# Batch 1's convolution on VectorE, batch 4's q by DMA transpose, convolution buffers of one batch, and a new written-out order

## The chip, the core and the metric

The kernel runs on one core of a Trainium2 chip. A core has five engines with an instruction queue each: TensorE (PE, with its weight loads as PEld), VectorE (DVE), ScalarE (ACT), GpSimd (POOL) and SyncE (SP). Each runs its own instructions in order; they wait for each other by semaphores. Transfers run on 16 DMA engines that POOL's and SP's queues share. The metric is the time of one execution on the device in microseconds (us).

## The reference

```python
kv  = einsum('bhsd,bhse->bhde', k, v)         # 8 batches, 8 heads, 576 rows, 64 wide
out = einsum('bhsd,bhde->bhse', q, kv)
x   = out / sqrt(mean(out * out, -1) + 1e-6) * g_norm   # heads side by side: 576 x 512
h   = maximum(x @ w_in, 0)                    # 576 x 1024
conv = conv_w[0] * h[s-1] + conv_w[1] * h[s] + conv_w[2] * h[s+1]   # along the rows
result = (h * sigmoid(conv)) @ w_out          # 576 x 512, float32
```

q, k, v and the weights arrive as float32 in HBM; the kernel computes in bfloat16 and sums in float32.

## The kernel before, in words

All eight batches pass through the same steps, and the steps of different batches lie beside each other. The program is one list of tokens, `ORDER` (from line 67). A loop at the end of the kernel calls one small function for each token, in the order of the list, so that the list fixes each engine's own order of instructions. A token is the function's name with its arguments (`hm.2.5`: batch 2, slice 5), `@` and the numbers of the buffers it takes, and `:1` or `:0`, which chooses between ScalarE and VectorE where a function has both.

The steps of a batch b, with their functions and the lines of their instructions:

- `Lq`, `Lk`, `Lv` (L301): POOL issues a load of the whole batch, 576 KB in bfloat16, cast on the way. Each of q, k and v has two buffers in turn, by the number behind `@`, so a load waits until what was in its buffer has been read (q of 7 takes the buffer of q of 4). `Li` and `Lo` (L315, L322) load the weights.
- `kv` (L358): 48 matmuls for k by v, with tiles of 128 by 64. `kvc` (L341, L343) copies the result out; from batch 4 on it is `kvn`, and the half that has to change partitions comes by a second copy (`ky`) or by DMA (`kx`, L449).
- q transposed. Batches 0 to 3: `qt` (L380) on TensorE, then a copy `qc`. Batch 4: `qtp`, the same step through `by_parity`, 24 transposes of two heads' worth each (L388), then `qc` on VectorE. Batches 5, 6, 7 (`QD`, line 60): `dq`, two DMA transposes a batch, four heads each, that SP issues (L436); no TensorE, no copy.
- out: `ot` (L430, L431) for batches 0 to 3, `oq` (L464) from batch 4 on, with tiles of 64 by 64, one for each pair of heads. `oq.b.0` and `oq.b.1` need the transpose `dq.b.0`; `oq.b.2` and `oq.b.3` need `dq.b.1`.
- the norm: `sq` squares (ScalarE), `oc` copies out, `ss` (L575, tiles of 128 by 32) sums, `ln` and `sl` make the factors, `sp` (L603, tiles of 32 by 128) spreads them, `mu` (L629) multiplies into x. Batch 7 spreads them through HBM instead (`fw`, `fr`).
- `hm` (L640): 8 matmuls of 288 columns for each of 8 slices of h; `re` evicts one with the maximum (L646 on ScalarE, L648 on VectorE).
- the convolution, in groups of batches (`CONV`, line 64): 0 and 1 alone, then 2 with 3, 4 with 5, 6 with 7. `ta` (L699, L700) makes the two outer taps, `aa` (L706) and `ab` (L712) add, all on VectorE; `sg` (L745) takes the sigmoid on ScalarE; `mg` (L751) multiplies it into h on VectorE. For slices 6 and 7 of batches 0 and 1 the convolution is instead a matmul with diagonal weights, `cm` (L731), and `sg` reads its result (L742). The buffers are two tiles `taps`, each for two slices of two batches.
- `om` (L761): h by w_out, 128 rows and 8 matmuls of 512 columns for each output row block; `ea` evicts it, `st` (L795) stores it through SP. The last block is done in halves (`oh`, L776).

`unread` (L427) runs matmuls on a constant whose result nobody reads.

Around the change, SP's queue is in the order of its tokens: transposes, `kx`, factors and stores. POOL's queue holds all loads in one line.

Of the kernel before, what the change touches and what calls it, by code (L numbers as in the profile page):

```python
# [72 lines left out]
sqh.0.3.0@3 unread.3@3 onh.0.3.0@6 sqh.0.3.1 onh.0.3.1 nlh.0.3.0@3 muh.0.3.0 Lk.1.0@1 qt.1.0@0 nlh.0.3.1 qc.1.0:1@2
muh.0.3.1 Li.0 hm.0.2@6 re.0.2 ta.0.2@0 hm.0.3@4 re.0.3 hm.0.6@6 Lq.1.2 ta.0.3 Lv.1.2 re.0.6 aa.0.1 hm.0.7@4 Lk.1.2
Lq.2.0@0 cm.0.6@6 re.0.7:1 sg.0.6@1 kv.1.0.2@0 cm.0.7@4 kvc.1.0.2.0:1@1 kvc.1.0.2.1 sg.0.7 ot.1.0@0 hm.0.1@6 ab.0.1
sq.1.0@4 re.0.1 qt.1.1@4 hm.0.0@2 on.1.0@6 mg.0.3 qc.1.1@3 ot.1.1@4 nl.1.0@4 re.0.0:1 sq.1.1@5 kv.1.2.2@2
kvc.1.2.2.0 ta.0.0@1 mu0.1.0 kvc.1.2.2.1 on.1.1@6 Li.2 ot.1.2@2 nl.1.1@5 ot.1.3@0 ta.0.1 sq.1.2@6 mu0.1.1 aa.0.0
unread.1@6 on.1.2@6 sq.1.3@7 ab.0.0 nl.1.2@6 mu0.1.2 on.1.3@4 nl.1.3@7 Lk.2.0@0 qt.2.0@6 sg.0.3 qt.2.1@4 mu0.1.3
ha.1.2@2 hb.1.2 qc.2.1@4 sg.0.2 qc.2.0@0 ha.1.3@0 hb.1.3 re.1.2 re.1.3 hm.1.7@4 Lv.2.0@0 hm.0.4@2 mg.0.1 Lq.3.0@1
hm.0.5@0 sg.0.1 Lk.3.0@1 Lv.3.0@1 re.1.7 sg.0.0 pl ta.1.2@0 re.0.4 ta.1.3 re.0.5 hm.1.4@4 kv.2.0.4@2 Lo.0 aa.1.1  # L80
ab.1.1 mg.0.0 sg.1.3 sg.1.2 kvc.2.0.4.0@0 hm.1.5@0 kvc.2.0.4.1 ta.0.4@1 ta.0.5 ot.2.0@2 mg.1.1 aa.0.2 hm.1.6@6
re.1.4 ot.2.2@4 re.1.5 sq.2.0@0 ta.1.4@0 ab.0.2 re.1.6 qt.3.1@0 oc.2.0:1@0 qt.3.0@6 qc.3.1@1 hm.1.1@2 ot.2.1@0
# [35 lines left out]
om.3.0.0@4 st.2.3 ea.3.6@6 ea.3.1@0 st.3.6 st.3.3 st.3.1 st.2.4 st.2.5 om.3.5.4 om.3.2.4 om.3.7.0@2 st.2.6 ea.3.4@6
st.2.0 eh.3.8.0@7 st.3.4 om.3.0.4 ea.3.5@0 om.3.7.4 oh.3.8.1 ea.3.2@3 ea.3.0@4 ea.3.7@1 st.3.5 st.1.4 sh.3.8.0
st.3.2 st.3.0 st.3.7 eh.3.8.1 sh.3.8.1  # L120
"""


# [722 lines left out]
```

## Time and profile before

| | us |
|---|---|
| median of 3 runs (179.9 to 182.42) | 180.41 |
| span of the profiled execution | 177.6 |
| around it, to the median | 2.8 |
| PE busy | 168.4 |
| ACT busy | 149.7 |
| DVE busy | 139.5 |
| POOL busy | 30.8 |

The span runs from the first to the last instruction. "Busy" is the time in which the engine had an instruction in work. The profile's rows of digits cut the span in 40 slices of 4.4 us and give the busy share of each in tenths. The chain of waits follows the work that ended last back to what released it. In the timeline a row stands for instructions in sequence: start, time, engine, line and operation, and their number; the duration of a single matmul overlaps with the next one's, so that what a matmul adds is read from starts, or from the chain. For a transfer, "to landing" is the time from its issue to its last byte. The rows of DMA queues give packets, megabytes, and the time of the packets as a share of 16 engines: q0 holds POOL's casting loads, q1 what SP issues.

### The profile page before, as it was taken

To read this page: it belongs to the slowest core of one execution; us is meant where nothing else is said; L and a number is where in the kernel's file an instruction comes from. 1 tells how busy PE (TensorE), PEld (TensorE's weight loads), DVE (VectorE), ACT (ScalarE), POOL (GpSimd) and SP (SyncE) were. 2 spreads that over 40 slices of the span, in tenths; PEclk is the share of its full clock that TensorE was granted. 3 is DMA by queue.
4 is the path that set the end of the run, shared out by engine and by line. 5 is a ranking of instruction groups with operands and counts; after the bars stand their busy time and mean duration, and the time that the engine had idled before them with its cause. 6 is when DMAs were issued, how large, how long until landed. Compare 5 with 4: busy or idle time off the path is not lost.

```text
span 177.6 us, 4060 instructions
## 1 busy us (share of the span) xinstructions
PE 168.4 (95%) x1641; PEld 101.3 (57%) x1660; DVE 139.5 (79%) x235; ACT 149.7 (84%) x233; POOL 30.8 (17%) x54
## 2 busy tenths in 40 slices
PE   6989996999999999999999999999999999999992
PEld 2545753877545677753667764444677764444541
DVE  5665669999998898999799999939999999950000
ACT  2479899999999969999999999999989987764332
POOL 7995516402600013050000000000000000000000
PEclk9999999999999999999999999999999999999999
DMA  6999999999999999999999950197040003422696
GB/s 155 188 183 197 200 204 201 205 203 206 205 204 203 198 192 139 174 203 198 160 201 179 293 128 0 53 219 263 21 160 0 4 0 143 152 82 99 258 352 219
DMA packets 36219, 29.49 MB, mean 166 GB/s; under 512 B 8528, under 2 KB 31720, under 8 KB 36200
## 3 DMA queue, kind: packets, MB, share of 16 engines
q0 software_dynamic: 21760, 15.96, 59.5%
q1 hardware_dynamic: 14400, 13.26, 28.9%
q8 instruction: 13, 0.21, 0.4%
q14 instruction: 6, 0.05, 0.1%
q10 hardware_dynamic: 40, 0.01, 0.0%
HBM read 33.70 MB, written 9.58 MB: 244 GB/s over the span
## 4 chain that ended last, share of the span: by engine, by line
PE 70%; DMA 20%; POOL 4%; ACT 2%; issue 2%; POOLq 0%; ACTq 0%
PE bank L761 33%; PE bank L640 27%; DMA v_sb<-in_v_dram 10%; DMA k_sb<-in_k_dram 7%; DMA q_sb<-in_q_dram 4%; PE bank L358 3%; PE bank L464 2%; POOL q_sb L241 1%; PE bank L603 1%; PE bank L575 1%; POOL v_sb L241 1%; POOL k_sb L241 1%; PE bank L776 1%; PE bank L731 1%; PE bank L388 1%
## 5 line engine op out<-in xcount | busy, mean ns | idle before, releaser
L640 PE MATMUL bank<-xT,w_in_sb 128*128 128x288 bf16 x496 | 64.5, 286 | 0.1
L761 PE MATMUL bank<-w_out_sb,h 128*128 128x512 bf16 x268 | 63.0, 379 | 1.1 <-issue 0.6
L640 PEld LDWEIGHTS <-w_in_sb 128*128 128x128 bf16 x496 | 47.6, 98 | 14.1 <-issue 0.5
L761 PEld LDWEIGHTS <-h 128*128 128x128 bf16 x280 | 26.3, 98 | 30.6 <-issue 1.9
L646 ACT ACTIVATE h<-bank 128x576 bf16<-128x576 f32 x61 | 37.9, 657 | 4.2 <-PE bank L640 3.9
L745 ACT ACTIVATE taps<-taps,cwn 128x1152 bf16<-128x1152 bf16 (+1 forms) x36 | 38.2, 1094 | 0.1
L341 ACT ACTIVATE row<-bank 128x512 f32<-128x512 f32 (+1 forms) x37 | 21.3, 598 | 12.3 <-PE bank L761 9.3
L751 DVE TENSOR_TENSOR h<-h,taps 128x2304 bf16<-128x2304 bf16 (+1 forms) x20 | 22.2, 1113 | 2.0 <-ACT taps L745 1.2
L706 DVE TENSOR_TENSOR taps<-taps 128x2304 bf16<-128x2304 bf16 (+1 forms) x18 | 20.9, 1160 | 0.4
L712 DVE TENSOR_TENSOR taps<-taps,h 128x2304 bf16<-128x2304 bf16 (+1 forms) x18 | 20.8, 1153 | 0.3
L699 DVE TENSOR_SCALAR taps<-h,cwn 128x1152 bf16<-128x1152 bf16 (+1 forms) x36 | 16.7, 463 | 2.5 <-ACT h L646 2.4
L493 ACT ACTIVATE sq<-bank 128x576 bf16<-128x576 f32 x28 | 17.9, 676 | 0.0
L700 DVE TENSOR_SCALAR taps<-h,cwn 128x1152 bf16<-128x1152 bf16 (+1 forms) x36 | 17.5, 487 | 0.0
L629 DVE SCALAR_TENSOR_TENSOR xT<-o,cw,bank 128x576 bf16<-128x576 f32 x20 | 15.3, 809 | 2.7 <-PE bank L603 2.5
L341 ACT ACTIVATE o<-bank 128x576 f32<-128x576 f32 x22 | 15.0, 694 | 0.0
L213 ACT ACT_TABLE_LOAD x10 | 12.8, 1283 | 2.5 <-issue 2.4
L301 POOL DMA_DIRECT2D q_sb<-in_q_dram x8 | 6.2, 772 | 31.4 <-PE bank L388 16.6
L427 PE MATMUL bank<-fill 128*128 128x512 bf16 x25 | 9.0, 480 | 1.7 <-DVE fill L228 1.5
L358 PEld LDWEIGHTS <-k_sb 96*64 96x64 bf16 x384 | 7.3, 114 | 4.0 <-issue 2.6
L358 PE MATMUL bank<-v_sb,k_sb 96*64 96x64 bf16 x384 | 8.5, 199 | 1.0 <-DMA k_sb<-in_k_dram 0.7
L301 POOL DMA_DIRECT2D k_sb<-in_k_dram x8 | 6.1, 758 | 14.4 <-PE bank L358 12.5
L562 DVE SCALAR_TENSOR_TENSOR xT<-bank,cw,root 128x576 bf16<-128x576 f32 x7 | 5.6, 815 | 1.8 <-ACT root L542 1.7
(93 smaller groups left out, 135.3 us busy)
## 6 DMA issues: line engine op xcount, KB each, us to landing
out_dram<-row SPq DMA_DIRECT2D x35, 256.0 KB, 2.8
q_sb<-in_q_dram POOLq DMA_DIRECT2D x6, 576.0 KB, 13.7
k_sb<-in_k_dram POOLq DMA_DIRECT2D x6, 576.0 KB, 14.7
v_sb<-in_v_dram POOLq DMA_DIRECT2D x6, 576.0 KB, 16.3
factor<-factor SPq DMA_DIRECT2D x4, 288.0 KB, 4.9
w_in_sb<-in_moe_w_in_dram POOLq DMA_DIRECT2D x4, 256.0 KB, 8.7
w_out_sb<-in_moe_w_out_dram POOLq DMA_DIRECT2D x2, 512.0 KB, 18.0
q_sb<-in_q_dram POOLq DMA_DIRECT2D x4, 144.0 KB, 4.6
```

The lines of the kernel that those rows point to most:

```text
L341: nc.scalar.activation(to, fr, AX.Copy)
L358: nc.tensor.matmul(ps[i][i * D:(i + 1) * D, t - t0, :], k_sb[:, 2 * t + i, r * D:(r + 1) * D], v_sb[:, 2 * t + i, r * D:(r + 1) * D], star ...
L493: nc.scalar.activation(in_order(b, s), product(b, t), AX.Square)
L640: nc.tensor.matmul(ps[:, e, :HS], w_in_sb[:, t, f * P:(f + 1) * P], x[:, t, e * HS:(e + 1) * HS], start=(t == 0), stop=(t == NT - 1))
L646: nc.scalar.activation(to, fr, AX.Relu)
L699: nc.vector.tensor_scalar_mul(tap[:, 0, f % 2, :n, 8:8 + S], h[:, f], cwn[:, 0, f:f + 1])
L700: nc.vector.tensor_scalar_mul(tap[:, 1, f % 2, :n, :S], h[:, f], cwn[:, 2, f:f + 1])
L706: nc.vector.tensor_add(tap[:, 1, :, :n, :S], tap[:, 0, :, :n, 7:7 + S], tap[:, 1, :, :n, 1:1 + S])
L712: nc.vector.tensor_add(y, y, h[:, 2 * j:2 * j + 2])
L745: nc.scalar.activation(y, y, AX.Sigmoid, scale=cwn[:, 1, f:f + 1])
L751: nc.vector.tensor_mul(h, h, T["tap", c, j][:, 1, :, :n, :S])
L761: nc.tensor.matmul(T["om", p, m], h[:, f, m * P:(m + 1) * P], w_out_sb[:, f, :], start=(f == 0), stop=(f == NF - 1))
```

## The change

Three edits, and a new `ORDER` for all of the list.

- Batch 1's convolution of slices 6 and 7 is done as the other slices are, by `ta`, `aa` and `ab` on VectorE; the tokens `cm.1.6` and `cm.1.7` go.
- Batch 4 joins `QD`: its q is transposed by two DMAs, `dq.4.0` and `dq.4.1`; the tokens `qtp.4.0`, `qtp.4.1`, `qc.4.0` and `qc.4.1` go.
- The two tiles `taps` for two batches become four units for one batch each; a group of one batch takes one unit, a group of two takes two that lie side by side.

The new list also moves work between ScalarE and VectorE by the `:` choices (16 evictions of `hm` on VectorE, before 3; seven output rows there, before none), places 25 instead of 27 `unread` matmuls, and changes TensorE's tile shape 71 times instead of 80. Loads stand in the order v4, k4, q4, q5, k5, v5, q7, k6, v6, k7, v7, q6 (before: q4, q5, k4, v4, k5, v5, q7, v7, k7, k6, v6, q6), and SP's queue begins with `dq.4.1`, `dq.4.0`, `dq.5.0`, `st.0.3`, `dq.5.1` (before: `dq.5.0`, `dq.5.1`, `st.0.0`, `dq.7.0`).

```diff
-QD = (5, 6, 7)
-QP = (4,)
+QD = (4, 5, 6, 7)
+QP = ()
...
+    def units(n):
+        s = slots.pop(0)
+        return taps[:, s:s + n].rearrange("p b k f w -> p k f b w")
...
-    taps = [consts.tile([P, 2, 2, 2, TW], BF16, name=f"taps{i}") for i in range(2)]
+    taps = consts.tile([P, 4, 2, 2, TW], BF16, name="taps")
...
-        for t in taps:
-            nc.vector.memset(t[:, 0, :, :, 7:8], 0.0)
-            nc.vector.memset(t[:, 1, :, :, S:S + 1], 0.0)
+        nc.vector.memset(taps[:, :, 0, :, 7:8], 0.0)
+        nc.vector.memset(taps[:, :, 1, :, S:S + 1], 0.0)
...
-            T["tap", c, f // 2] = taps[slots.pop(0)]
+            T["tap", c, f // 2] = units(CONV[c][1])
...
-                T["tap", c, f // 2] = taps[slots.pop(0)]
+                T["tap", c, f // 2] = units(CONV[c][1])
```

Of the list, the stretch around batch 4 and the line with `kv.7`:

```diff
-dq.5.0@3 ea.0.1@0 mu.2.1.0 Lk.5.0@1 mu.2.1.1 om.0.0.4 ea.0.3@1 ln.1@0 sp.2.0@4,6 mu.2.0.1 mu.2.0.0 dq.5.1@0
-om.0.2.0@2 Lv.5.0@1 sg.1.5 sg.1.4 qtp.4.0@0 cm.1.6@6 qc.4.0@4 mg.1.2 ea.0.0@2 hm.2.5@4 sl.1@0 hm.2.2@0 sg.1.1
...
-mu.4.1.1 sp.4.0@4,0 kv.7.0.4@6 mu.4.0.0 sg.2.2 mu.4.0.1 om.0.7.4 kvn.7.0.4:1 sg.2.3 ea.0.7@2 sp.5.0@4,2 hm.3.0@0
...
+om.0.3.0@0 mu.2.0.1 mu.2.1.0 dq.4.1@2 al.x2@0 mu.2.1.1 sl.1@0 om.0.3.4 ea.0.3@3 hm.2.2@4 kv.4.0.4@0 sg.1.2 ab.1.3
+re.2.2 sp.3.0@2,6 mu.3.0.0 sg.1.4 sg.1.7 Lq.5.0@1 mu.3.0.1 hm.2.6@4 kvn.4.0.4 ky.4.0.4.0 ky.4.0.4.1 Lk.5.0@1 re.2.6
+sg.1.6 hm.2.3@2 hm.2.7@6 aa.1.0 sp.3.1@0,4 re.2.3:1 dq.4.0@0 hm.2.5@2 ab.1.0 dq.5.0@1 Lv.5.0@1 st.0.3 re.2.7 sg.1.1
+sg.1.5 mu.3.1.1 hm.2.4@6 re.2.5 mu.3.1.0 mg.1.3 dq.5.1@3 hm.3.4@4 re.2.4:1 oq.4.2@0 sg.1.0 mg.1.2 re.3.4 sq.4.2@0
...
+st.0.2 sp.4.0@0,4 kv.6.0.4@3 kv.7.0.4@7 mu.4.0.0 mu.4.0.1 sg.2.2 sp.4.1@0,4 ea.0.7@1 kvn.6.0.4:1 hm.2.1@2 mu.4.1.0
```

More of the change, by code (lines that the diff above doesn't have):

```diff
@@ L73 @@
[L73 to L82, printed above, removed]
@@ L118 @@
[L118 to L120 removed]
+pre@0,0,0 ca.v.0 unread.10@6 qt0.0.0@0 ca.k.0 kv.0.0.1@1 kvc.0.0.1.0@0 kvc.0.0.1.1:1 qc0.0.0:1@0 pi Lq.1.0@1 Li.3
+qt0.0.1@2 unread.2@6 ot.0.0@4 kv.0.1.1@3 al.h1@0 ct@0 sq.0.0@0 on.0.0@6 kvc.0.1.1.0:1 qc0.0.1:1 nl.0.0@0 pg unread.2@0
@@ new lines @@
+qt0.0.2@1 al.h0@1 al.x0@0 Li.1 kvc.0.1.1.1:1 ot.0.1@2 pc sq.0.1@0 unread.3@6 kv.0.2.1@0 on.0.1@6 qc0.0.2@1 nl.0.1@1
+mu0.0.0 kvc.0.2.1.0:1 pn Lv.1.0@1 kvc.0.2.1.1 dg.6:1 unread.2@4 qt0.0.3@1 mu0.0.1 ot.0.2@4 unread.2@7 kv.0.3.1@0,6
+sq.0.2@0 Lk.1.0@1 on.0.2@2 qc0.0.3 kvc.0.3.1.1:1 kvc.0.3.1.0 Li.0 ot.0.3@0 Lk.1.2 nl.0.2@0 sqh.0.3.0@0 sqh.0.3.1
+unread.3@6 onh.0.3.0@6 Lq.1.2 onh.0.3.1 mu0.0.2 dg.7:1 nlh.0.3.0@1 qt.1.0@2 muh.0.3.0 nlh.0.3.1 muh.0.3.1 hm.0.7@4
+qc.1.0@0 hm.0.6@0 Lv.1.2 hm.0.2@2 re.0.6:1 ps hm.0.3@6 re.0.7 Li.2 Lk.2.0@0 cm.0.6@0 kv.1.0.2@4 re.0.2:1 re.0.3:1
@@ new lines @@
+sg.0.6@0 kvc.1.0.2.0@0 kvc.1.0.2.1 cm.0.7@2 ta.0.2@1 ot.1.0@0 ta.0.3 al.x1@1 aa.0.1 sg.0.7 sq.1.0@0 hm.0.0@4 hm.0.1@2
+mg.0.3 on.1.0@6 re.0.0:1 nl.1.0@0 re.0.1 Lv.2.0@0 qt.1.1@4 ot.1.1@6 kv.1.2.2@2 ab.0.1 sq.1.1@0 Lq.2.0@0 qc.1.1@1
+on.1.1@4 kvc.1.2.2.0 kvc.1.2.2.1 ot.1.3@2 ta.0.0@0 mu0.1.0 nl.1.1@1 Lq.3.0@1 ot.1.2@0 pl hm.0.4@4 sq.1.3@0 Lv.3.0@1
+Lk.3.0@1 ta.0.1 sq.1.2@1 mu0.1.1 on.1.2@6 nl.1.2@0 re.0.4:1 on.1.3@4 mu0.1.2 hm.0.5@6 ha.1.2@0 nl.1.3@1 mu0.1.3
+hm.1.5@4 aa.0.0 ta.0.4@2 sg.0.3 re.0.5 sg.0.2 hm.1.4@2 hm.1.0@6 ab.0.0 Lo.0 hb.1.2 ta.0.5 re.1.4:1 hm.1.1@2 re.1.5
@@ new lines @@
+re.1.2 qt.2.1@0 kv.2.0.4@4 aa.0.2 Lo.1 ab.0.2 sg.0.1 sg.0.0 re.1.0:1 sg.0.4 kvc.2.0.4.0@0 qt.2.0@6 qc.2.1@0 Lv.4.0@0
+re.1.1 kvc.2.0.4.1 ha.1.3@0 mg.0.0 hb.1.3 ot.2.2@2 qc.2.0@1 sg.0.5 sq.2.2@0 hm.1.7@4 ot.2.0@6 oc.2.2@0 sq.2.0@1
+oc.2.0@1 mg.0.1 re.1.3:1 hm.1.6@0 qt.3.1@2 re.1.6 ot.2.1@6 ta.1.4@3 ot.2.3@0 re.1.7 ta.1.5 Lk.4.0@0 ta.1.0@0 qt.3.0@4
+mg.0.2 sq.2.1@2 sq.2.3@3 qc.3.1@1 ta.1.2@1 ss.2@2 ta.1.3 ln.8@0 unread.1@3 kv.3.0.4@3 kvc.3.0.4.0@0 kvc.3.0.4.1
+ot.3.2@2 qc.3.0@0 aa.1.2 oc.2.1:1 ot.3.1@4 ot.3.0@6 oc.2.3 om.0.0.0@0 om.0.1.0@1 sq.3.2@0 sq.3.0@1 aa.1.1 Lq.4.0@0
@@ new lines @@
+oq.5.3@4 sq.5.3@6 ab.2.1 sq.5.1@7 om.0.5.4 om.0.4.0@6 mg.2.2 ss.4@7 ta.2.6@2 ss.5 ea.0.6@2 om.0.8.0@0 oc.5.3 oc.5.1
+hm.3.0@4 Lv.7.0@1 ln.2@0 ta.2.7 re.3.0 ea.0.5@3 aa.2.3 sl.2@0 om.0.7.0@2 om.0.8.4 ea.0.8@4 ab.2.3 om.0.7.4 om.0.4.4
+st.0.2 sp.4.0@0,4 kv.6.0.4@3 kv.7.0.4@7 mu.4.0.0 mu.4.0.1 sg.2.2 sp.4.1@0,4 ea.0.7@1 kvn.6.0.4:1 hm.2.1@2 mu.4.1.0
+sg.2.3 mu.4.1.1 al.h2@1 dq.7.1@4 hm.4.2@0 mg.2.1 dq.7.0@0 ea.0.4@5 re.2.1 kvn.7.0.4 kx.6.0.4.0 sp.5.1@4,2 hm.4.1@6
+re.4.2 mu.5.1.1 kx.7.0.4.0 hm.4.3@0 kx.6.0.4.1 sg.2.6 hm.4.5@2 mu.5.1.0 re.4.1 re.4.3 Lq.6.0@1 re.4.5 sp.5.0@0,4
@@ new lines @@
+hm.4.0@6 ta.2.0@0 ta.2.1 hm.4.4@2 mu.5.0.1 mu.5.0.0 re.4.0 kx.7.0.4.1 hm.5.2@4 aa.2.0 hm.4.7@0 sg.2.7 ab.2.0 mg.2.3
+hm.5.3@6 re.5.2 hm.5.1@4 re.4.4 re.4.7 hm.5.0@0 sg.2.1 re.5.3:1 oq.7.0@2 sg.2.0 re.5.1:1 re.5.0 oq.7.1@6 hm.5.5@4
+hm.5.4@0 mg.2.0 ta.3.2@2 st.0.6 sq.7.0@0 oc.7.0@0 re.5.4:1 re.5.5 sq.7.1@1 om.1.0.0@2 oc.7.1 ta.3.3 aa.3.1 dq.6.0@1
+oq.7.2@0 ea.1.0@2 st.0.8 oq.6.0@4 sq.7.2@2 oq.7.3@6 ab.3.1 oc.7.2:1@1 om.1.3.0@3 om.1.6.0@2 sq.7.3@3 sq.6.0@4
+ea.1.3:1@4 dq.6.1@2 oc.7.3 oq.6.3@0 ea.1.6:1@6 st.1.0 oq.6.2@6 oc.6.0@2 ta.3.4@0 sg.3.3 oq.6.1@4 om.1.5.0@3 sq.6.1@5
@@ new lines @@
+sq.6.3@6 ss.7@2 sq.6.2@7 oc.6.1:1 oc.6.2@3 ta.3.5 sg.3.2 oc.6.3 ln.4@0 ss.6@4 st.0.4 hm.4.6@6 re.4.6 ea.1.5@2
+om.1.1.0@5 fw.4 st.1.5 aa.3.2 hm.5.7@0 mg.3.1 om.1.2.0@2 ea.1.1@5 ta.3.0@2 ta.3.1 hm.5.6@6 re.5.7 al.x3@1 ab.3.2
+om.1.8.0@3 ln.3@0 sl.3@0 fr.7.0@0 re.5.6 sp.6.0@0,4 aa.3.0 mu.6.0.0 mu.6.0.1 ea.1.2@2 om.1.7.0@2 sp.6.1@0,6 ea.1.8@7
+om.1.4.0@3 mu.7.0.0 mu.6.1.0 fr.7.1@1 mu.6.1.1 hm.6.0@0 mu.7.1.1 mu.7.1.0 st.1.6 sg.3.4 hm.6.6@4 ab.3.0 sg.3.5 al.h3@0
+mu.7.0.1 st.0.5 mg.3.2 ea.1.4@3 st.1.4 re.6.0 hm.6.2@0 re.6.6 hm.6.1@4 hm.6.3@6 re.6.2 ea.1.7@3 ta.3.6@0 sg.3.1 re.6.3
@@ new lines @@
+st.1.8 ta.3.7 hm.6.4@0 hm.7.3@2 re.6.4 re.7.3 re.6.1 hm.7.0@0 aa.3.3 hm.6.7@2 hm.7.2@4 hm.7.7@6 sg.3.0 ab.3.3 mg.3.0
+st.1.7 st.0.0 re.6.7 re.7.2 re.7.0:1 hm.7.1@2 hm.6.5@0 sg.3.6 sg.3.7 ta.4.2@2 ta.4.3 mg.3.3 ta.4.0@0 re.7.1 ta.4.1
+hm.7.6@4 aa.4.1 ab.4.1 re.7.7 hm.7.4@2 om.2.7.0@6 re.7.6 ea.2.7@0 hm.7.5@4 re.6.5 aa.4.0 om.2.0.0@6 sg.4.2 sg.4.3
+om.2.8.0@7 st.1.1 ab.4.0 om.2.5.0@0 mg.4.1 ta.4.6@2 re.7.4 ta.4.7 om.2.3.0@1 st.1.2 aa.4.3 sg.4.1 sg.4.0 st.0.7 st.2.7
+om.2.2.0@2 om.2.6.0@3 ea.2.5@0 mg.4.0 om.2.1.0@0 ea.2.2@1 re.7.5 ea.2.8@2 ta.4.4@0 ea.2.0@3 ta.4.5 ab.4.3 aa.4.2
@@ new lines @@
+sg.4.6 om.3.7.0@2 om.2.4.0@4 ea.2.6:1@5 ea.2.1@6 om.3.4.0@5 om.3.3.0@0 sg.4.7 ea.2.4@7 st.2.6 ab.4.2 om.3.2.0@3 sg.4.5
+st.2.4 st.1.3 om.3.6.0@4 st.2.8 st.2.0 sg.4.4 om.3.1.0@6 mg.4.3 om.3.5.0@7 ea.2.3@5 mg.4.2 om.3.6.4 om.3.4.4 om.3.7.4
+ea.3.4:1@2 st.2.2 st.2.5 om.3.3.4 om.3.1.4 om.3.5.4 st.2.3 st.3.4 om.3.2.4 ea.3.3:1@0 ea.3.7@7 ea.3.6@1 ea.3.1:1@3
+st.3.3 ea.3.5@4 om.3.0.0@2 om.3.0.4 st.3.7 st.3.1 ea.3.2@2 st.3.5 oh.3.8.0@0 oh.3.8.1 eh.3.8.0@0 st.2.1 ea.3.0:1@5
+st.3.6 st.3.2 st.3.0 eh.3.8.1 sh.3.8.0 sh.3.8.1
```

43 lines of the change are left out of this document (6 added, 37 removed).

## The prediction

> **What bounds the kernel now.** Four views, in this order. The page first:
>
> ```profile
> span 177.6 us, 4060 instructions
> ...
> PE 168.4 (95%) x1641; PEld 101.3 (57%) x1660; DVE 139.5 (79%) x235; ACT 149.7 (84%) x233; POOL 30.8 (17%) x54
> ...
> PE   6989996999999999999999999999999999999992
> ...
> DVE  5665669999998898999799999939999999950000
> ...
> DMA  6999999999999999999999950197040003422696
> ...
> q0 software_dynamic: 21760, 15.96, 59.5%
> ```
>
> Two resources are full. TensorE is at 9 from the eighth slice on; the DMA engines are at 9 until slice 23 (about 100 us), and what fills them is q0, the casting loads that POOL issues. Then the chain in order of time shows where the one hands over to the other:
>
> ```profile
> 28.67 17.11 DMA v_sb<-in_v_dram
> 45.78 0.14 issue
> 45.91 0.95 PE bank L358 x48
> ...
> 63.94 0.88 PE bank L358 x48
> ...
> 88.23 0.88 PE bank L358 x48
> ...
> 96.88 0.88 PE bank L358 x48
> ```
>
> L358 is the k-by-v product of a batch (`kv`). Up to 45.8 us the chain is loads: `kv` of batch 3 starts as its v lands. After that it is TensorE to the end, and 45.9 to 174.3 holds only small gaps. The other rows are `kv` of batches 4, 7 and 6; that of 5 is at 75.96. They start late enough for their loads. The question for this change is whether that stays so. Then the transposes by DMA (L436), SP's timeline with the time that its queue took over each, and over all six the time to landing:
>
> ```profile
> 56.40 7.41 SPq L436 DMA_TRANSPOSE qT<-q_sb  x2
> ...
> 78.24 1.51 SPq L436 DMA_TRANSPOSE qT<-q_sb  x1
> ...
> 91.06 1.33 SPq L436 DMA_TRANSPOSE qT<-q_sb  x1
> ...
> 95.14 1.47 SPq L436 DMA_TRANSPOSE qT<-q_sb  x1
> ```
>
> ```profile
> DMA to landing us min/median/max: 4.2/10.7/16.0
> ```
>
> One by one, from issue to landing: 10.7 (56.4), 16.0 (58.3), 12.0 (78.2) while loads run; 5.2 (91.1) and 4.2 (95.1) when the loads are ending. Last, what one does to the loads, from the DMA view of 46 to 60 us (no transpose) and of 82 to 90 us (one, on q1):
>
> ```profile
> q0 software_dynamic: 3580, 2.85, 129.6%
> ```
>
> ```profile
> q0 software_dynamic: 1450, 1.09, 95.3%
> q1 hardware_dynamic: 1184, 0.30, 37.7%
> ```
>
> 2.85 MB in 14 us is 0.204 MB/us, so a 576 KB load (0.59 MB) needs 2.9 us. In 8 us that would be 1.63 MB; 1.09 were moved. One transpose costs the loads 0.54 MB, 2.65 us. The 15 us from 60 agree: 1.68 of 3.06 MB, 6.8 us lost to two transposes and one 256 KB store (1.3 us).
>
> **The change, part by part.** The sum is made against the profiled execution: span 177.6, and 2.8 us around it give the median of 180.4.
>
> *TensorE work removed after batch 3's `kv`.* Two `cm` of batch 1 (L731): 0.74 + 0.85 us on the chain. 24 transposes of batch 4 (L388): 0.51 + 0.62. Three fills there, of which the trace shows two (L427): 0.32 + 0.38; the new ones stand ahead of `kv`. `ss` of batch 2 goes ahead of it: 0.36. Changes of tile shape fall from 80 to 71, all nine after `kv`: on the chain eight matmuls of `om` take 1.73 us among their like, and four take 0.97, not 0.87, where another shape follows, so 0.1 us each, 0.9. Together 4.7 us. Ahead of `kv` the work grows by 0.3, and its loads land when they did, so I count 0.3 against: 4.4 us.
>
> *VectorE and ScalarE.* Two `ta` pairs, one `aa` and one `ab` for f 6 and 7 of batch 1: 4 x 0.38 + 0.76 + 0.75 = 3.0 us of VectorE; their sigmoids on ScalarE are 0.78 instead of 0.65. Two copies of q (0.75 each) leave VectorE. 13 more evictions of `hm` (net) run there at 0.75 instead of ScalarE at 0.66, seven of the 35 whole output rows too. By start-to-start intervals VectorE has 9.4 us more between `kv` of batch 3 and its last product: eight evictions 5.3, three output rows 1.8, two copies of o 1.3, and 1.0 net of batch 1's convolution against q's copies. It was idle for 9.3 us from 46 to that product's end at 158.9, so it just fits; priced as a rival. The buffers in one-batch units cost nothing by themselves: four memsets (62 ns) become two, and no shape changes. What they allow is the new order.
>
> *q of batch 4 by DMA.* Loads are now v4, k4, q4, q5, k5, v5, q7, k6, v6, k7, v7, q6. The third load after w_out landed at 59.2 before (k of batch 4: 44.2 + 15.0), so q4 lands at 59.2. Summing intervals over the new order, `oq.4.2` stands 18.3 us behind `kv` of batch 3, `oq.4.1` 22.6, `oq.5.2` 26.6, `kv` of 6 and 7 37.6 and 38.4. The old order sums to 40.5 where the trace has 42.3 (45.9 to 88.2), so I add up to 1.8 for small gaps: 65.4, 69.7, 73.8, 85.4, 86.2 us.
>
> The first transpose, `dq.4.1`, heads SP's queue: issue at 59.2, landing 10.7 later, 69.9, as q5, k5 and v5 are streaming beside it. `oq.4.2` waits 4.5 us at the head of TensorE's order, and everything behind it does. `dq.4.0` follows by between 3.1 (landings at 96.3 and 99.3) and 7.2 us (67.1 and 74.3): 73 to 77; `oq.4.1` would be at 74.2, up to 2.9 more. `dq.5.0` and `dq.5.1` queue behind: another 1 to 4 us at `oq.5.2`.
>
> SP's stores behind (`st.0.3`, `st.0.1`, `st.0.2`) and the `kx` of batches 6 and 7 are later too; the first free row buffers that are asked for 10 us and more later, the second have the 13 us to `oq.7.0` (98), and both keep that cover, since TensorE is late as well: nothing.
>
> Those waits are not yet the worst. POOL's load of q7 needs batch 4's q buffer. It waited for a transpose on TensorE until 65.7 (the 16.6 us of "POOL q_sb L301 <- PE bank L388" among the waits); now for the landing of `dq.4.0`, 73 to 77, with k6, v6, k7, v7 and q6 behind it in POOL's queue. q5 lands at 62.1, k5 and v5 after 4.1 us each (62.7 to 66.8 is what a load took beside a transpose), so v5 has landed by about 70 and the stream runs dry. The first load of the kernel landed 4.2 us after issue and its 0.15 MB move in 0.7, so data flow 3.5 us after an issue: 76.5 to 80.5. Five loads are 14.5 us, plus one to three transposes beside them (`dq.5.1`, `dq.7.1`, `dq.7.0`) at 2.65: v7 lands at 93.6 to 103. The order puts `kv` of batch 7 directly behind that of 6, at 86.2; before, the last `kv` was at 96.9 and its v landed at 92.6. I take v7 at 97, as some transposes fall into the dry stretch. TensorE is then 11 us behind (the waits at `oq` are part of it), and all that follows is TensorE work.
>
> Sum: 180.4 - 4.4 + 11 = 187.0. With v7 at 93.6 or 102: 183.5 or 192.
>
> [...]
>
> [...]
>
> **The rivals.**
> - *Faster: transposes land as the late ones did* (4.2 to 5.2 us, 3.1 apart). `dq.4.1` lands at 64, `dq.4.0` at 67, q7 is issued before v5 lands, the stream has no hole, and v7, the eighth load from 59.2, lands at 82.4 and a little more. Then only the 4.4 us count: 176.0. For it: 4.2 at 95.1. Against: all three beside running loads took over 10. It decides if `dq.4.1` lands by 65.4 and v7 by 87. 8%.
> - *A transpose takes only its bytes' share*, 1.45 us, and the stream stays fed: eight loads from 59.2 are 23.2 us, six transposes 8.7; v7 at 91.1, 4.9 us late, 180.9. Against: 0.54 MB lost in 82 to 90 us. 16%.
> - *Loads are in time, VectorE is the bound.* If it keeps all 9.3 us of idleness beside 9.4 of added work, its last product ends at 168.3 instead of 158.9, with 9.6 us of TensorE and 3.3 of tail behind: 181.2 of span, 184.0. If it keeps none, 176.0. Middle: 180. For it: VectorE's digits, nearly all 9. 11%.
> - *The waits also slow the array.* The first ten fills took 4.45 us, 0.43 each, against 0.216 later, and full pace came 5.6 us after the first: about 2.8 us lost. One such loss on top of mine: 189.8; two, 192.6. Between 46 and 174 no wait is long enough to tell. 13%.
>
> **How the numbers follow.** Mine has 52%: 187.0, its own range 183.5 to 191.5. A measurement of this kernel can tell about 2% from no change: below 176.8 is faster, above 184.0 slower. Faster: 8%. Within: 16 + 11, and 5 of mine at its lower end, 32%. Slower: 47 + 13, 60%. From 179.5 to 191.5 it leaves out the faster case and about half of the last, and takes in the others.
>
> **What would show it.** Right: L436 landings over 10 us for the first two; a PE wait for them near 65 us and another at `kv` (L358), for v_sb, near 86 to 97; POOL's q_sb waiting for a DMA, not PE; DMA digits dropping below 9 near 70 to 77; no L388 or `cm` of batch 1; PE busy some 4 us shorter. Wrong: TensorE without a gap past 46 us, or the first transpose landing within 6 us, or POOL's last loads landing by 87. If DVE idles under 3 us from 46 on while PE waits for L751, it is the third rival. Granted clock under 1.00 behind a wait: the fourth.

## The result, and the profile after

The changed kernel takes 191.38 us (median of 4 runs, 188.9 to 191.83), the kernel before 180.17 (179.9 to 182.42) on the same chip: a ratio of 1.060, 95% interval 1.052 to 1.0675. Medians and ranges here and below are of all runs of a kernel; ratios leave out a run that lies more than 1.5% above the fastest of its kernel. The profiled execution took 191.22 us, its span 189.3, 11.7 more than before.

The page of the changed kernel, with the lines that answer to those of before:

```profile
span 189.3 us, 4018 instructions
...
PE 171.4 (91%) x1622; PEld 101.5 (54%) x1622; DVE 153.6 (81%) x255; ACT 139.7 (74%) x215; POOL 30.8 (16%) x54
...
PE   6899998999899909999879999999789999999991
...
PEclk9999999999999996999966999999999999999998
DMA  6999999999999999999991900306937001006685
```

TensorE now has three thin places: a digit 0 (66 to 71 us), an 8 7 (90 to 99) and a 7 8 (132 to 142). At the first two the granted clock shows a 6, once and twice; at the third it doesn't. The DMA engines are full until 99 us (102 before). TensorE is busy for 3.0 us longer although it has 38 matmuls fewer. The half clock behind the first two (0.55 and 0.50 in the windows below) explains part of that; besides, the trace of before has records of only 1641 of its 1660 matmuls (its weight loads, PEld, count 1660), so its 168.4 us are too short. What TensorE waited for (us in total, times, longest):

```profile
PE bank L466 <- DMA qT<-q_sb: 4.3, 1, 4.3
PE bank L360 <- DMA v_sb<-in_v_dram: 2.1, 1, 2.1
```

L466 is the product `oq` of batch 4's q, L360 the product `kv` (L358 before). The chain in order of time, from 59 to 106 us (start, length, what), joins the two waits:

```profile
59.13 11.48 DMA qT<-q_sb
70.62 0.04 issue
70.66 0.44 PE bank L466 x8
71.10 5.70 PE bank L642 x32
...
79.36 16.61 DMA v_sb<-in_v_dram
95.97 0.04 issue
96.01 1.50 PE bank L360 x26
...
97.87 3.95 PE bank L642 x16
```

The transpose `dq.4.1` is issued as q of batch 4 lands (59.13) and lands itself at 70.62; v of batch 7 lands at 95.97. Sixteen matmuls of L642 (`hm`) take 3.95 us behind the second wait. At full pace they take 2.1 (below, in the run with batch 7's transposes later). The windows show the clock that was granted (start:end, length, busy time of PE, PEld, DVE, ACT and POOL, then PEclk, DMA share, GB/s):

```profile
73.00:75.40 2.40, 2.40 (x12) 1.56 (x11) 2.15 (x3) 1.67 (x4) 1.48 (x2) 0.55 0.95 115
...
95.60:99.00 3.40, 2.99 (x58) 2.23 (x58) 1.09 (x2) 0.76 (x2) 0.00 (x0) 0.50 1.42 159
99.00:102.50 3.50, 3.50 (x18) 1.88 (x17) 1.91 (x3) 1.57 (x4) 0.00 (x0) 0.51 0.15 27
```

POOL's timeline shows the load of q7 held back by a transpose, as forecast, and ScalarE's a wait that nobody forecast:

```profile
72.19 0.77 POOL L303 DMA_DIRECT2D q_sb<-in_q_dram  x1 [22.07 <-DMA qT<-q_sb]
```

```profile
139.07 0.60 ACT L343 ACTIVATE row<-bank 128x512 f32<-128x512 f32 x1 [2.78 <-DMA out_dram<-row]
```

That evacuation (`ea.1.4`) needs the row buffer that the store `st.0.5` empties, and the order issues this store on SP only behind `fr.7`, the copies of batch 7's table. `hm.6.2` needs a bank that ScalarE empties behind it. Beneath this lies a second wait at the same place: VectorE's queue has a `mu` of batch 7 ahead of two of batch 6, so it waits for that table, and TensorE waits for VectorE at `hm.6.0`:

```profile
136.02 0.82 DVE L627 SCALAR_TENSOR_TENSOR xT<-o,cw,factor 128x576 bf16<-128x576 f32 x1 [1.95 <-DMA factor<-factor]
```

```profile
PE bank L642 <- DVE xT L631: 1.5, 1, 1.5
```

Where the time went is read by setting the start of each group of matmuls in the trace against the sum of the intervals of the work ahead of it at full clock. By these sums the new order has 4.2 us less work. It falls behind them by 26.0 us to the end, the old order by 10.8. The difference of 15.2 is, in order: 0.7 up to `kv` of batch 3, 1.0 at `ot.3.2` just behind it, 4.35 at `oq.4.2`, 1.8 at half clock, 2.3 at `kv` of batch 7, 2.5 at half clock, 2.3 from `hm.6.0` to `hm.6.2` where the two waits just shown lie over each other, and small ones. 15.2 - 4.2 = 11.0, of the 11.7 that the span grew.

### The profile page after: what moved, and what is told of

It reads as the page before. It is cut to its first block, busy times and chain, and to the rows that moved or that the text cites. A ratio compares the mean times of both kernels' runs of the same rounds, so it can differ in the third digit from the quotient of the medians.

```text
span 189.3 us, 4018 instructions
## 1 busy us (share of the span) xinstructions
PE 171.4 (91%) x1622; PEld 101.5 (54%) x1622; DVE 153.6 (81%) x255; ACT 139.7 (74%) x215; POOL 30.8 (16%) x54
## 4 chain that ended last, share of the span: by engine, by line
PE 51%; DMA 31%; ACT 5%; DVE 5%; issue 3%; POOL 2%; SPq 2%; POOLq 0%; ACTq 0%
PE bank L642 24%; PE bank L763 18%; DMA v_sb<-in_v_dram 11%; DMA q_sb<-in_q_dram 9%; DMA qT<-q_sb 6%; DMA out_dram<-row 3%; PE bank L360 2%; ACT L216 1%; SPq L619 1%; DMA factor<-rs 1%; PE bank L778 1%; PE bank L466 1%; PE bank L382 1%; PE bank L733 1%; ACT root L544 1%
## 5 line engine op out<-in xcount | busy, mean ns | idle before, releaser
L642 PE MATMUL bank<-xT,w_in_sb 128*128 128x288 bf16 x496 | 68.9, 296 | 2.0 <-DVE xT L631 1.5
L763 PE MATMUL bank<-w_out_sb,h 128*128 128x512 bf16 x280 | 63.8, 379 | 0.0
L642 PEld LDWEIGHTS <-w_in_sb 128*128 128x128 bf16 x496 | 49.2, 101 | 19.8 <-issue 4.4
L747 ACT ACTIVATE taps<-taps,cwn 128x1152 bf16<-128x1152 bf16 (+1 forms) x38 | 39.8, 1075 | 3.0 <-DVE taps L714 2.9
L648 ACT ACTIVATE h<-bank 128x576 bf16<-128x576 f32 x48 | 30.4, 650 | 11.1 <-PE bank L642 10.4
L343 ACT ACTIVATE row<-bank 128x512 f32<-128x512 f32 (+1 forms) x30 | 16.9, 582 | 16.0 <-PE bank L763 6.0
L701 DVE TENSOR_SCALAR taps<-h,cwn 128x1152 bf16<-128x1152 bf16 (+1 forms) x38 | 17.8, 468 | 4.6 <-ACT h L648 4.6
L702 DVE TENSOR_SCALAR taps<-h,cwn 128x1152 bf16<-128x1152 bf16 (+1 forms) x38 | 17.9, 471 | 0.0
L343 ACT ACTIVATE o<-bank 128x576 f32<-128x576 f32 x21 | 13.6, 669 | 0.0
L650 DVE TENSOR_SCALAR h<-bank 128x576 bf16<-128x576 f32 x16 | 11.9, 751 | 2.0 <-PE bank L642 1.4
L360 PE MATMUL bank<-v_sb,k_sb 96*64 96x64 bf16 x384 | 8.9, 203 | 2.4 <-DMA v_sb<-in_v_dram 2.1
L360 PEld LDWEIGHTS <-k_sb 96*64 96x64 bf16 x384 | 7.9, 118 | 4.8 <-issue 4.5
L345 DVE COPY row<-bank 128x512 f32<-128x512 f32 x7 | 4.8, 688 | 6.1 <-PE bank L763 5.8
```

Of the source, the lines that this page charges most:

```text
L343: nc.scalar.activation(to, fr, AX.Copy)
L360: nc.tensor.matmul(ps[i][i * D:(i + 1) * D, t - t0, :], k_sb[:, 2 * t + i, r * D:(r + 1) * D], v_sb[:, 2 * t + i, r * D:(r + 1) * D], star ...
L642: nc.tensor.matmul(ps[:, e, :HS], w_in_sb[:, t, f * P:(f + 1) * P], x[:, t, e * HS:(e + 1) * HS], start=(t == 0), stop=(t == NT - 1))
L648: nc.scalar.activation(to, fr, AX.Relu)
L747: nc.scalar.activation(y, y, AX.Sigmoid, scale=cwn[:, 1, f:f + 1])
L763: nc.tensor.matmul(T["om", p, m], h[:, f, m * P:(m + 1) * P], w_out_sb[:, f, :], start=(f == 0), stop=(f == NF - 1))
```

## The experiments

In the first four, theory A is mine: two transposes beside the loads, with q7's load behind them. Ratios are to the kernel before on the same chip, with 95% intervals. The rounds ran on different chips, where the kernel before took 179.3 to 180.2 us, so a difference of two medians below is good to about 1 us. The edits are edits of `ORDER`.

**Q of batch 4 on TensorE again, in the changed kernel.**

```diff
-QD = (4, 5, 6, 7)
+QD = (5, 6, 7)
+QP = (4,)
-... dq.4.1@2 ... dq.4.0@0 ... hm.3.4@4 re.2.4:1 oq.4.2@0
+... qtp.4.1@0 qc.4.1@2 hm.3.4@4 re.2.4:1 qtp.4.0@2 qc.4.0@0 oq.4.2@0
```

> The changed kernel with one part undone: q of batch 4 is transposed on TensorE again (sixteen transposes and two PSUM copies), the new order and the convolution on VectorE stay. Theory A (the two early DMA transposes and the q7 load that queues behind them cause the waits, and each wait is followed by half-clock work): no wait at the q k product of batch 4, the load of q7 starts near 67 us instead of 72.2, v7 lands some 5 us earlier, its wait is under 1 us or gone, the clock stays at 1.0; 4.4 + 1.8 + 2.3 + 3.4 us go and 1.5 to 2.5 us of transposes, copies and shape changes come back: 181.5 us, between 180 and 185. Rival B (the new order itself is the slow part: its loads of batch 7 and the early kv of batch 7 come too late with or without the transposes): 187 us or more, with a wait of 2 us or more at the kv product of batch 7. Rival C (VectorE with the whole convolution is the bound): 187 us or more and no DMA wait of over 1 us on TensorE.

Measured: 185.33 us (183.95 to 188.85), 1.027 (1.021 to 1.034). So some 6 us of the change hang on this one part. (The edit brings back 24 transposes, not sixteen.) But a wait stays:

```profile
75.20 17.69 DMA v_sb<-in_v_dram
92.93 0.95 PE bank L360 x48
```

v7 lands 3 us earlier than in the changed kernel, not 5, TensorE waits 2.5 us for it, and the clock falls behind it (0.72 from 95 to 100 us). 185.33 is at the end of A's range (185), and the wait at `kv` of batch 7 is B's sign: A explains half of the loss, and something in the loads of batches 6 and 7 is left, with q of batch 4 out of it.

**Only q of batch 4 by DMA, in the kernel before.**

```diff
-... oc.3.3 sp.2.1@6,0 ss.3@5 dq.5.0@3 ... qtp.4.0@0 ... qc.4.0@4 ... qtp.4.1@6 ... qc.4.1@2
+... oc.3.3 sp.2.1@6,0 ss.3@5 dq.4.0@4 dq.4.1@2 dq.5.0@3 ...
```

> The kernel before with only q of batch 4 sent by DMA transpose (issued ahead of the transposes of batch 5); order and convolution as before. Theory A: the two transposes beside the loads land 10 to 12 us after issue; the load of q7, which reuses the buffer of q4, starts near 71 us instead of 63, k7 and v7 some 5 us later than before, and TensorE waits 2 to 5 us at the q k product of batch 4 or at the kv product of batch 7; 184 us, between 182 and 188. Rival B (only the new order pays for it): the 1.1 to 1.3 us of transposes taken from TensorE are gained, 179 us, at most 180.4.

Measured: 186.29, 186.63 and 186.62 us, and once 182.39; no interval is given for so uneven a set. It is slower than before in every run, with the order and the convolution untouched, so rival B's 179 is out. The profile is of one of the three; that the run of 182.39 has the same wait isn't shown. The wait came at another place than A said:

```profile
PE bank L463 <- DMA kvx<-kvn: 4.3, 1, 4.3
```

`kvx` is the 2 us copy of batch 7's kv; it took 7.28 us (93.87 to 101.15) beside the last load and a transpose. Here the late load stream reaches a transfer that it did not meet before.

**Only the convolution's last slices on VectorE, in the kernel before.**

```diff
-... cm.1.6@6 qc.4.0@4 mg.1.2 ea.0.0@2 ... sg.1.6@0 ... sp.3.0@6,4 cm.1.7@0
+... qc.4.0@4 mg.1.2 ta.1.6@0 ta.1.7 aa.1.3 ab.1.3 ea.0.0@2 ... sg.1.6 ... sp.3.0@6,4
```

> The kernel before with only the last two slices of batch 1's convolution moved from TensorE to VectorE; order and transposes as before. Theory A (VectorE has room for its 3 us and TensorE is freed of 1.59 us): 179.2 us, between 178.5 and 181. Rival C (VectorE is the bound there): 181.5 us or more, with TensorE waiting on VectorE by 1 us or more more than before. The q4 transposes are on TensorE, so no wait on a DMA at the q k product under either.

Measured: 182.15 us, 1.013 (1.008 to 1.018). A's gain isn't there, C's number is. One wait of TensorE carries it:

```profile
PE bank L602 <- DVE wparts L593: 2.8, 1, 2.8
```

VectorE's timeline shows why: the six operations take 58.07 to 60.8 us, and the four that make the spreading weights (`wparts`) come behind them, at 62.54 instead of 60.2.

**The two waits of the changed kernel filled with work.**

```diff
-re.2.4:1 oq.4.2@0 ... kv.6.0.4@3 kv.7.0.4@7
+re.2.4:1 unread.18@0 oq.4.2@0 ... kv.6.0.4@3 unread.16@7 kv.7.0.4@7
```

> The changed kernel with TensorE kept busy in its two DMA waits: 18 fill matmuls, whose results nobody reads, ahead of the waiting q k product of batch 4, and 16 ahead of the kv product of batch 7. Theory A (the half clock follows from the idle wait and is a cost of its own): the granted clock stays at 1.0 through both places and 1.8 us after the first wait and 2.5 to 3.4 us after the second are won back: 186.5 us, between 185 and 188. Rival D (the loads set the time, so work regained after the first wait is lost at the second, and the low clock costs nothing of its own): 189.5 us or more, with a longer wait at the kv product of batch 7. If the fills fall where there is no wait, they cost up to 3.9 us each.

Measured: 190.82 us, 1.063 (1.058 to 1.067), level with the changed kernel. The clock did what was wanted; the same windows:

```profile
73.00:75.40 2.40, 2.40 (x24) 1.77 (x25) 2.22 (x3) 2.28 (x6) 1.79 (x3) 1.00 0.95 121
...
95.60:99.00 3.40, 2.20 (x58) 1.45 (x57) 0.15 (x1) 0.00 (x0) 0.00 (x0) 1.00 1.27 191
99.00:102.50 3.50, 3.50 (x32) 2.46 (x30) 3.50 (x5) 2.42 (x4) 0.00 (x0) 1.00 0.37 64
```

Twice as many matmuls fit into 73.0 to 75.4 us (24 for 12), and yet nothing is won in the end: v7 landed at 97.59, later than without the fills (95.97), and TensorE waited for it all the same. Behind that it was 1.1 us ahead of the changed kernel, at `hm.6.0` 2.1, and at `hm.6.2`, behind ScalarE's wait for the store (3.4 us here), 0.5. So the half clock behind the first wait costs nothing by itself here, since the next wait takes it up. For the one behind the second wait this run settles nothing, as v7 moved too and the store's wait grew; the next run says more.

**The transposes of batch 7 later, in the changed kernel.**

```diff
-al.h2@1 dq.7.1@4 hm.4.2@0 mg.2.1 dq.7.0@0 ea.0.4@5 re.2.1 kvn.7.0.4 kx.6.0.4.0 sp.5.1@4,2
+al.h2@1 hm.4.2@0 mg.2.1 ea.0.4@5 re.2.1 kvn.7.0.4 kx.6.0.4.0 dq.7.1@4 dq.7.0@0 sp.5.1@4,2
```

> The changed kernel with the two DMA transposes of batch 7 moved on SP's queue from the place where q7's landing releases them (81.6 and 83.2 us) to behind the first copy of batch 6's kv (some 94 us); nothing else is changed. Theory E (transposes that run beside the loads slow the loads, and the landing of v7 holds TensorE at the kv product of batch 7): after q7 the loads come 2.8 us apart as they do between 20 and 46 us, v7 lands near 92.8 instead of 96.0, the wait of 2.1 us and the half clock behind it are gone, the transposes land by 102, ahead of the q k product of batch 7: 186.5 us, between 185 and 188.5. Rival F (the loads of batches 6 and 7 are slow for another reason, the transposes only share idle time): v7 at 95 or later, 190 to 191.5.

Measured: 186.41 us (185.8 to 187.16), 1.040 (1.035 to 1.044). Theory E had 186.5, F 190 or more. TensorE's timeline where the second wait was, all 96 matmuls of two `kv` in one go and sixteen `hm` at full pace:

```profile
94.19 1.71 PE L360 MATMUL bank<-v_sb,k_sb 96*64 96x64 bf16 x96
95.83 0.44 PE L605 MATMUL bank<-wparts,spread 32*128 32x288 bf16 x4
96.20 2.13 PE L642 MATMUL bank<-xT,w_in_sb 128*128 128x288 bf16 x16
```

The DMA view of 82 to 94 us, first of the changed kernel, then of this run (packets, MB, share):

```profile
q0 software_dynamic: 2561, 1.93, 103.1%
q1 hardware_dynamic: 1604, 0.40, 25.5%
```

```profile
q0 software_dynamic: 3226, 2.43, 131.1%
```

Without 0.40 MB of transposes the loads move 0.50 MB more in the same 12 us. From q7's landing to v7's, four loads, it is 11.6 us (82.39 to 93.99) instead of 14.4 (81.61 to 95.97). In these 14.4 us 0.50 MB of transposes moved, so that one of 0.295 MB costs 1.6 us of load time by this count and 1.8 by the megabytes of the 12 us. The wait of 2.3 us at `kv` and the half clock behind it both go. In the traces, `kv` of batch 6 starts 1.3 us later than in the changed kernel (94.19 and 92.93) and the run of 56 `hm` behind it 3.8 us earlier (101.85 and 105.61): together 5.0 us at this place. Not all of it is left at the end. The first wait stays, is longer in this profile (5.7 us at `oq.4.2`), and has 6.8 us of half clock behind it in place of 3.4; the spans differ by 4.4 us, the medians by 5.0, the ratios by 2.0%, or 3.6 us.

**A third buffer for q, in the changed kernel.**

```diff
-Lq.7.0@0
+Lq.7.0@2
```

> The changed kernel with a third buffer for q: the load of q7 goes into it and waits for no transpose. Theory G (the wait of q7's load for the transposes of batch 4 is what makes the loads late): q7 lands near 73.5 instead of 81.6, k6 and v6 before 80, v7 near 86 to 90, no wait at the kv product of batch 7 and no half clock behind it: 186 us, between 184.5 and 188; the wait of 4.3 us at the q k product of batch 4 stays, and may grow by up to 3 us, as the loads no longer pause. Rival E alone (the sharing with the transposes is the whole cost, the buffer wait none): the transposes of batch 4 land later by what the loads gain, 189.5 us or more.

Measured: 194.85 us, 1.085 (1.076 to 1.094), slower than the changed kernel. Theory G falls; rival E's number holds, and the transposes do land later by what the loads gain. The waits and the chain:

```profile
PE bank L466 <- DMA qT<-q_sb: 9.7, 2, 5.5
```

```profile
70.72 0.48 PE bank L466 x3
71.20 2.12 SPq L438
73.31 0.05 issue
73.36 0.57 SPq L797
73.94 0.06 issue
74.00 13.44 DMA qT<-q_sb
87.43 0.14 issue
87.57 0.70 PE bank L466 x7
```

q7 landed at 74.53 instead of 81.61. But the transposes of batches 4 and 5, which in the changed kernel landed at 70.62, 71.60 and 72.62, once the loads had stopped at 70.44, now landed at 70.67, 76.88, 83.27 and 87.43. (The trace doesn't have the landing of the fourth in the changed kernel.) The wait of q7's load had been the pause in which they got through. The last transpose stands behind two others and a store on SP's queue; that is what TensorE waits for at batch 5.

**One store earlier, in the changed kernel.**

```diff
-st.0.6 sq.7.0@0 ... mu.7.0.1 st.0.5 mg.3.2
+st.0.5 st.0.6 sq.7.0@0 ... mu.7.0.1 mg.3.2
```

> The changed kernel with one output store (row block 5 of the first pair) ahead of that of row block 6 on SP's queue, where its row has long been written, instead of behind the table load; nothing else is changed. Theory H (the evacuation that waits for this row buffer holds the gelu and TensorE by 2.3 us on the path that sets the end): 189 us, between 188 and 190. Rival I (the lost time is caught up before the end, since TensorE waits there for VectorE and ScalarE anyway): 191 us or more.

Measured: 189.47 us, 1.055 (1.050 to 1.060), three of four runs at 188.85 to 189.85. That is the size that H gives, but the interval overlaps that of the changed kernel: inconclusive by time. The profile is of the fourth run (194.25). In it the wait of ScalarE for that store is gone, and TensorE's wait for VectorE at `hm.6.0` is still there, as VectorE waits 2.1 us for batch 7's table:

```profile
PE bank L642 <- DVE xT L631: 1.7, 1, 1.7
```

By the sum of intervals TensorE loses 2.0 us between `hm.5.7` and `hm.6.2` in this profile, 2.4 in that of the changed kernel. So H's mechanism is not borne out: with the store out of the way, the wait beneath it costs nearly as much.

**Four moves at once.** Q of batch 4 on TensorE, batch 7's transposes later, the store earlier, and `kv.7.0.4@7` behind `hm.4.3@0`. In this kernel the product `kv` of batch 7 is written over a bank that still holds a hidden product of batch 4, so that part of the computation is changed.

> The changed kernel's order and its convolution on VectorE, with q of batch 4 on TensorE again, the transposes of batch 7 behind the first copy of batch 6's kv, the kv product of batch 7 some 5 us of TensorE work later, and the store of row block 5 earlier. Theory J (order and convolution are sound by themselves; what costs is the data that comes late): 185.3 us of the run with q of batch 4 on TensorE, less 2.7 and 1.6 us at the kv product, less 1.2 at the store, 180 us, between 178 and 182. Rival B (the order itself is slow, VectorE and ScalarE come late in it): 184 us or more, with no wait of TensorE on a DMA above 1 us.

Measured: 182.53 us, 1.0165 (1.012 to 1.021): between the two. No wait on a DMA is left (the longest wait that stands behind the start of the kernel is 1.2 us, on VectorE), which J wanted, but 2.5 us more than J gave. Neither theory has both; the next run takes one of the moves back.

**The order alone.** The same, with `kv` of batch 7 where the change has it.

> The changed order and its convolution on VectorE, with q of batch 4 on TensorE, the transposes of batch 7 behind the first copy of batch 6's kv, the store of row block 5 earlier, and the kv product of batch 7 where the change has it. Theory J (late data is the whole cost): v7 lands near 89, ahead of TensorE, no wait on a DMA above 1 us, the clock stays at 1.0: 181 us or less. Theory L (order and convolution cost some 3 us by themselves, in small waits on VectorE and ScalarE that the order before does not have): 182 to 183.5, with no wait on a DMA either.

Measured: 181.21 us, 1.008 (1.005 to 1.011), a little above J's end and below L's. (Not quite alone: batch 7's transposes stand later here than in the change, and the one store earlier.) v7 lands at 88.96; TensorE waits 0.6 us on a load. From the run with q of batch 4 on TensorE it is 4.1 us, nearly all of it the wait and the half clock at `kv` of batch 7. The page:

```profile
PE 167.1 (93%) x1630; PEld 100.6 (56%) x1646; DVE 155.1 (86%) x257; ACT 139.5 (78%) x215; POOL 30.4 (17%) x54
...
PEclk9999999999999999999999999999999999999999
```

So the order, with these two moves, and the convolution cost 1.4 us (0.5 to 1.1%), although TensorE has 3.2 us less to do by the sum of intervals: 4.6 us of small waits, such as 0.9 on ScalarE's copy of batch 3's kv and 0.7 on VectorE's copy of batch 4's q.

**The same with the convolution of two slices left out.** This kernel leaves out the taps, sums, sigmoids and product of batch 1's slices 6 and 7, so that its result differs there.

```diff
-ta.1.6@2 ta.1.7 aa.1.3 ab.1.3 sg.1.6 sg.1.7 mg.1.3
```

> The kernel of the run beside it (changed order, q of batch 4 on TensorE, transposes of batch 7 later) with the convolution of the last two slices of batch 1 left out altogether: 3.7 us less of VectorE's work and 1.5 us less of ScalarE's, nothing less on TensorE. Theory C (VectorE sets the pace there, so its convolution work is paid for): 1.5 us or more below the run beside it. Theory M (those waits come from the order, not from the amount of VectorE's work): within 0.7 us of it.

Measured: 181.2 us, 1.009 (1.007 to 1.012). 3.7 us less of VectorE's work change nothing. Theory C is out for the changed order with q of batch 4 on TensorE; the convolution on VectorE is free there.

**The convolution on VectorE once more in the kernel before, 10 us later.**

```diff
-mg.1.2 ta.1.6@0 ta.1.7 aa.1.3 ab.1.3 ea.0.0@2 ... qc.4.1@2 ta.2.4@1 ... sq.4.1@1 re.2.6 ... re.3.3 ... ab.2.2
+mg.1.2 ea.0.0@2 ... qc.4.1@2 ta.1.6@0 ta.1.7 ta.2.4@1 ... sq.4.1@1 aa.1.3 ab.1.3 sg.1.6 re.2.6 ... re.3.3 sg.1.7 ... ab.2.2 mg.1.3
```

> The kernel before with the last two slices of batch 1's convolution on VectorE, but put behind the evacuations for batch 3 and ahead of batch 2's convolution, instead of ahead of the spreading weights of batch 3. Theory N (the convolution's price in the old order was its place, ahead of the weights that TensorE waits for): the wait of 2.8 us is gone and TensorE keeps the 1.6 us of matmuls it is freed of: 178 us, between 177 and 179. Theory C (VectorE is full from 55 to 115 us, so 3 us more of it come out somewhere): 180.5 us or more, with TensorE waiting on VectorE by 1 us or more at another place.

Measured: 182.38 us, 1.017 (1.0135 to 1.0205). The wait on the weights is gone, and another has come:

```profile
71.18 0.78 ACT L744 ACTIVATE taps<-taps,cwn 128x576 bf16<-128x576 bf16 x1 [1.39 <-DVE taps L711]
71.86 1.17 ACT L645 ACTIVATE h<-bank 128x576 bf16<-128x576 f32 x2
```

ScalarE's sigmoid (`sg.1.6`) waits for VectorE's sum, and the evacuations of `hm` (L645) stand behind it; TensorE waits 1.7 us for them. Besides, the time of the matmuls taken from TensorE is gone earlier: `kv` of batch 4 starts at 63.95 us, before at 63.87, with gaps of 0.1 to 0.3 us where they stood. C's number came true at a place that C did not name: it isn't VectorE that TensorE waits for, but an engine that waits for VectorE with TensorE's next bank behind it. Whether a third place would be free wasn't tried.

**Three small waits moved, in the order alone.**

```diff
-kvc.3.0.4.1 ... qtp.4.1@0 qc.4.1@2 hm.3.4@4 re.2.4:1 qtp.4.0@2 qc.4.0@0 oq.4.2@0 ... fw.4 st.1.5 ... fr.7.1@1
+kvc.3.0.4.1:1 ... qtp.4.1@0 qtp.4.0@2 qc.4.1@2 qc.4.0@0 hm.3.4@4 re.2.4:1 oq.4.2@0 ... fw.4 ... fr.7.1@1 st.1.5
```

> The kernel of the run with the order alone (changed order, convolution on VectorE, q of batch 4 on TensorE, transposes of batch 7 later, 181.21 us), with three moves that touch small waits of TensorE: one half of the copy of batch 3's kv goes to VectorE (wait of 0.9 us on ScalarE), the second transpose group of batch 4 goes one hidden product earlier (0.7 us on VectorE), and one store goes behind the table load for batch 7 on SP's queue (0.7 us on VectorE, which waits there for that load). Theory M (what is left of the loss is such waits of place): 0.4 + 0.8 + 0.7 us less, 179.3 us, between 178.6 and 180.2, level with the kernel before. Rival L (each wait that goes is taken over by the next): 180.7 us or more.

Measured: 191.07 us, 1.059 (1.053 to 1.065). L's number holds and M's doesn't, but the run doesn't decide between them: two of the three moves made new waits, larger than those they were to remove. TensorE's waits, and ScalarE's timeline:

```profile
PE bank L763 <- ACT row L343: 6.4, 1, 6.4
...
PE bank L432 <- DVE kvbd L345: 1.4, 2, 1.0
PE bank L432 <- DVE o L345: 0.9, 1, 0.9
```

```profile
132.38 1.09 ACT L343 ACTIVATE row<-bank 128x512 f32<-128x512 f32 x2 [7.05 <-DMA out_dram<-row]
```

The store that I moved behind the table copies left its row buffer full for 7 us, ScalarE stood, TensorE stood 6.4 us, and 1.7 us of half clock followed (the mean granted clock of this execution was 0.97). The copy that went to VectorE put three new waits there in place of one on ScalarE, with 3.4 us of half clock behind them; at `hm.2.2` TensorE is 3.3 us further behind than in the run with the order alone. Only the transpose group moved earlier did what it should: the wait on VectorE's copy of q is gone. No version here beats the kernel before.

## Why the prediction was right, and where it was not

The direction held. The range held by 0.1 us, which is luck (191.38 in 179.5 to 191.5; two of the four runs, 191.53 and 191.83, lie outside). The value was 4.4 us low.

- **The first transpose.** Forecast 59.2 + 10.7 = 69.9 and a wait of 4.5 us; measured 59.13 + 11.48 = 70.62 and 4.3. That a transpose beside the loads takes some 10.7 us, as the first such row of before did, was the step that carried the prediction, and it held.
- **The transposes behind it.** "`dq.4.0` follows by between 3.1 ... and 7.2 us", up to 2.9 us more at `oq.4.1` and 1 to 4 at `oq.5.2`: failed. They landed 1.0 us apart, with no wait. I had the loads run dry at 70 and didn't apply it to them. The run with the third q buffer, where the loads don't stop, shows the step itself: 6.2 and 6.4 us apart, and a wait at `oq.5.2`.
- **What a transpose costs the loads.** "0.54 MB, 2.65 us": mis-sized. It is 0.50 MB for 0.40 MB of transposes, 1.6 to 1.8 us each. The second rival's 1.45 us is nearer, an estimate from the loads' rate (0.295 MB at 0.204 MB/us). What else slowed the loads from 82 to 90 us in the kernel before stays open.
- **v7 at 97.** Measured 95.97. The size was right by errors that cancel: q7 was issued earlier than forecast (72.2, not 73 to 77) and arrived more slowly (9.4 us from issue, where I had 3.5 + 2.9), and only the loads ran dry. Between 73.0 and 75.4 us they moved 0.03 MB, but transposes and stores kept the DMA digits at 9, so that this sign of being right did not show.
- **"TensorE is then 11 us behind ... and all that follows is TensorE work."** Failed, and this is where the 4.4 us come from (5.4, since v7 at 95.97 would have given 186.0). Behind the second wait came 2.5 us of half clock, the fourth rival's mechanism, and 2.3 us from `hm.6.0` to `hm.6.2`, where ScalarE waits for a store that I had not looked at and VectorE for batch 7's table.
- **The half clock.** The rival added 2.8 us per wait. The first drop cost 1.8 and is absorbed by the second wait; the second cost 2.5 by the sum of intervals, and in the run with batch 7's transposes later it goes together with its wait of 2.3 (5.0 us at that place). The clock fell behind the wait of 4.3 us (0.55 from 73.0 to 75.4 us) and behind that of 2.1 us alike (0.50 from 95.6 to 99.0 us).
- **TensorE's removed work.** 4.4 us forecast; 4.2 by the sum of intervals. The trace has the rows: `cm` 3.6 us before, 1.8 after, and no transposes of batch 4 (1.4). That PE busy would be some 4 us shorter did not come out: it is 3.0 us longer.
- **VectorE as the bound.** Refuted for the changed order with q of batch 4 on TensorE (3.7 us of its work left out, no change). The 1.4 us that order and convolution cost are waits of place.

The runs make a chain, in which the parts add up by construction: 5.0 us for batch 7's transposes beside the loads, 5.2 for batch 4's (186.41 to 181.21, one store earlier in it), 1.4 for order and convolution, together 11.6 of the 11.2 measured; by the ratios 3.6, 5.7 and 1.4. With batch 4's taken back first it is some 6 and 4.1, so the split hardly depends on the order. What stays open is which of the small waits is worth moving, since nearly every move that was tried made others or uncovered one.

## What to carry to other kernels

Work taken off a full engine and given to the DMA engines wasn't free here, where these were full too (batch 4's q alone, in the kernel before: 182.39 to 186.63 us against 179.3): ask which transfer will land later, and who stands first behind it. A buffer wait that looks like a loss can be the pause in which other transfers get through (194.85 us without it, 191.38 with it), and a transfer that is issued as soon as possible can be worth more when it is held back until the stream it disturbs is done (186.41 us with batch 7's transposes later). Price a move in a hand-written order by every queue it touches; one store put behind four table copies cost 6.4 us at an engine that has nothing to do with it.
